# The same steps in another order: the step list of an attention and mixture-of-experts kernel

## The chip, the cores and the metric

The kernel runs on one core of a Trainium2 chip. The metric is the device time of one execution in microseconds (us). Five engines take part, each with its own queue of instructions that it works off in order: PE (TensorE, matmuls), DVE (VectorE), ACT (ScalarE), POOL (GpSimd) and SP (SyncE, which here issues nearly all DMA transfers).

## The reference

Linear attention with positive features (batch 4, 8 heads, 576 tokens, 64 dimensions a head, 128 features), then two layers of experts. In each, a gate picks one of 8 experts for each of the 2304 tokens.

```python
def phi(x):
    proj = np.einsum('bhsd,md->bhsm', x, omega)
    h = proj - np.sum(x * x, axis=-1, keepdims=True) / 2.0
    h = h - np.max(h, axis=-1, keepdims=True)
    return np.exp(h) / np.sqrt(m)
kv = np.einsum('bhsm,bhsd->bhmd', k_p, v)          # k_p = phi(k * scale)
z = np.sum(k_p, axis=2)
num = np.einsum('bhsm,bhmd->bhsd', q_p, kv)         # q_p = phi(q * scale)
den = np.einsum('bhsm,bhm->bhs', q_p, z)[..., None] + 1e-06
x = num / den                                       # then (2304, 512)
# each expert layer: N = 2304, D = 512, E = 8, F = 1024
e_idx = np.argmax(x @ w_gate, axis=1)
for e in range(E):
    mask = e_idx == e
    h = np.maximum(x[mask] @ w1[e], 0.0)
    out[mask] = gate_w[mask, None] * (h @ w2[e])    # layer 1: also * sigmoid(x @ w_output_gate)[:, e]
```

## The kernel before, in words

Attention works on 16 pairs of heads, four to a batch. The expert layers work on eight units, one for each layer and batch, in the order (layer 0, batch 0), (0,1), (1,0), (1,1), (0,2), (0,3), (1,2), (1,3). A unit runs the batch's most frequent expert over all 576 tokens. For precision each weight and each activation is split into a high and a low part and each product is three matmuls. Tokens whose expert is another one are left over; here they fit in one small block of 32, which is computed apart and added into the outputs.

**The step list.** Nothing in the program but the string `PLAN` (line 47) sets the order. A loop takes its words one after the other and issues what each names; so the list gives each engine's queue its order, and an engine waits when the next instruction of its queue is not ready. Instructions on different engines run at the same time as far as their data allow. A digit issues so many steps of the experts' stream; a step is six matmuls on PE (line 91). A unit has 64 steps, called here `E0.0` to `E7.63` (unit, then step). The first 32 go up: after every second step ScalarE makes `hh` (line 514) and VectorE `hl` (line 515) out of one of two PSUM buffers, which PE needs again. The other 32 go down: after every fourth step VectorE multiplies a buffer by the gate weights into `y` (line 533).

A word with `+` does its copy on VectorE, without it on ScalarE (line 128). The letters, p standing for the pair (a hexadecimal digit):

| word | what it issues |
|---|---|
| `ap`, `bp`, `cp` | SP: loads of q, k, v of the pair |
| `qp`, `r`, `t`, `s`, `x` | PE projects q; copies of it to `qhh`; POOL's maximum over partitions (`qhl`, line 225); VectorE subtracts (line 229); ScalarE's exp |
| `kp`, `m`, `e`, `v`, `w` | PE projects k; VectorE's row maximum `nm` (line 194); ScalarE's exp; PE's k v sums; copy `kvr` |
| `n`, `d`, `f`, `g`, `h`, `l`, `o` | PE's numerator; VectorE divides; PE transposes; copy `xraw`; high copy, low part, store |
| `Fui`, `Hui`, `Lui` | SP loads piece i of unit u's weights (512 KB into one of two `wr` buffers); copy to `wh`; VectorE's `wl` (line 487) |
| `Gu`, `Pu`, `Wu` | the gate of unit u in eleven parts; its expert's number to SP; the load of gate weights |
| `Xuc`, `Yuc`, `Suc0` | high copy, low part for the next layer; store of a piece of `y` |
| `A` | the left-over block in 34 parts: VectorE's scans pick its tokens (lines 627 to 649: `scan`, `scan2`, `sel`), POOL gathers, PE computes (`pu`, `pyc`, `pby`), VectorE scales (`yw`), POOL scatters in eight copies (`by`, line 731) |
| `B` | the block added into an output that is already stored: loads, four adds on VectorE (line 752), stores |
| `Mucs` | the block added into a piece of unit 7's `y`, on VectorE (line 547); its store `S` follows |
| `I`, `J`, `T`, `zn` | set-up; loads of the gates; pools changed; n idle matmuls on PE |

The block belongs to one of two places, and a factor of one or zero decides whether `B` or `M` adds it; both are issued. `B` and `M` need all eight `by` copies. A wait of an instruction holds all that stands behind it on its engine.

Of the kernel before, what the change touches and what calls it, by code (L numbers as in the profile page):

```python
# [46 lines left out]
PLAN = """
a0 I a1 b0 b1 c0 c1 c2 J a2 a3 a4 b2 b3 b4 b5 c3 c4 c5 q00 q01 k00 r001 r010+ k01 r000 t00 r011+ m00 t01 q10 r101+
e000 e001 m01 r100+ s00 z8 q11 e010 e011 r111 r110 k10 x00 m10 k11 s01 t11 m11 v00 v01 e100 q20 x01 w0+ r201+ e101
r200 e110 s11 e111 t10 n00 n01 q21 k20 a5 r211 r210 d00 d01 s10 x11 m20 v10 v11 x10 t20 f00 w1 e201 g00+ f01 k21 g01+  # L50
o0 m21 h0+ e200 s20 t21 q30 e211 e210 r301 r300 n10 n11 v20 v21 q31 x20 a6 s21 d10 k30 d11 w2 m30 r311 t31 l0 r310 x21
k31 q40 r400 r401+ e300 e301 t30 m31 n20 n21 e311 q41 e310 a7 d20 s31 r411 f10 g10 s30 f11 k40 x31 g11+ o1 m40 t41
r410 x30 d21 v30 v31 s41 h1 l1 e401 e400 k41 m41 b6 t40 w3 f20 g20 x41 f21 k50 g21 o2 m50 s40 e411 e410 n30 n31 v40
v41 c6 e500 h2+ e501 l2 w4 q50 q51 a8 x40 r500 r501 d30 r510 d31 r511 n40 n41 f30 d40 d41 g30 f31 k51 g31 b7 m51 o3 h3
t50 s50 t51 G0 e510 G0 e511 l3 k60 k61 G0 v50 v51 m60 e601 w5 G0 x50 b8 c7 e600 s51 x51 m61 G0 G0 z3 k70 e610 e611 G0
m70 P0 F00 F01 k71 m71 n50 v60 v61 e700 n51 c8 e710 e711 G0 w6 e701 d50 d51 f40 f41 G0 G0 G0 g40 g41 o4 v70 v71 f50
f51 H00+ L00 F02 g50 g51+ o5 W0 q60 q61 a9 H01 r600+ r611 r610+ 1 L01 F03 1 t60 2 s60 1 H02 1 x60 1 L02 F04 6 H03 1
L03 F05 2 H04 2 L04 F06 5 H05+ 1 L05 F07 3 H06+ c9 1 L06 3 w7 2 H07 1 L07 6 S000 1 r601+ 1 t61 2 s61 2 q70 q71 r711 aa
x61 r710 r701+ r700 1 t71 1 S010 n60 n61 s71 t70 d60 d61 1 x71 1 s70 1 h4+ 1 x70 l4 f60 f61 n70 n71 d70 d71 g60+ g61+
o6 h5 l5 2 f70 g70 f71 q80 q81 r801 ab g71+ G1 G1 o7 r800 r810 h6+ l6 h7+ l7 r811 1 G1 t80 G1 1 t81 S020 G1 G1 2 s80  # L60
G1 2 x80 P1 F10 F11 1 s81 1 G1 2 q90 q91 ac r911+ r910 S030 G1 G1 G2 H10+ G2 L10 F12 r900 k80 k81 H11 m81 t90 G2 1
e811 e810 L11 F13 1 s90 2 x90 2 H12 2 H13 L12 F14 2 L13 F15 7 H14+ 1 L14 F16 1 H15 2 L15 F17 6 H16 1 L16 4 H17 X00+
Y00 2 L17 1 m80 G1 W1 2 e800 e801 3 v80 v81 ca w8 X10 S100 X01 Y01 1 Y10 X02+ 3 Y02 X03 Y03 2 G2 1 r901+ 1 G2 G2 S110
t91 1 X11+ 1 G2 1 Y11 P2 F20 F21 s91 b9 1 G2 1 x91 2 x81 1 G2 n80 n81 X12 H20 Y12 d80 S120 G2 d81 1 L20 F22 1 H21+ 1
f80 f81 k90 k91 m90 L21 F23 m91 g80 g81+ o8 1 e900 e901 2 e911 e910 ba bb 2 S130 H22 1 L22 F24 X13+ 2 H23+ Y13 1 L23
F25 qa0 qa1 ka0 ra00 ad ra10 ka1 bc ta0 ma1 ma0 ra11+ ra01 1 ea11 ea10 1 sa0 ea00 ea01 1 ta1 1 H24 xa0 v90 v91 va0 va1
cb cc L24 wa F26 sa1 w9 kb0 kb1 kc0 mc0 xa1 mb1 bd mb0 1 ec01 ec00 1 eb10 eb11 1 eb01 eb00 G3 G3 n90 n91 na0 na1 vb0
vb1 d90 da0 da1 d91 cd qb0 qb1 ae rb10+ rb11+ rb00 rb01 wb 1 f90 f91 kd0 kd1 g90 g91 kc1 mc1 be tb0 sb0 o9 tb1 md1 bf
md0 1 ec11 1 xb0 sb1 fa0 ga0+ ed10 ed11 1 ed00 ed01 1 H25+ 2 fa1 qc0 qc1 af L25 F27 rc11 rc00+ ga1+ oa rc10 rc01 2 tc1
1 tc0 1 sc1 2 H26+ 1 xc1 sc0 ec10 1 L26 6 h8 H27+ 2 L27 l8 h9 l9 ha 1 la G2 W2 5 S200 8 S210 1 G3 G3 1 G3 G3 2 P3 F30  # L70
F31 G3 xb1 2 G3 1 nb0 nb1 G3 G3 G3 qd0 qd1 rd11 db0 db1 rd01+ rd10 rd00 1 fb0 S220 gb0+ H30 td1 fb1 1 H31 L30 F32 1
L31 F33 sd1 3 xd1 gb1+ ob 1 hb lb 2 H32 W3 S230 G4 G4 L32 F34 1 H33+ G4 G4 L33 F35 1 G4 G4 3 G4 1 P4 2 G4 vc0 vc1 vd0
vd1 G4 H34 ke0 L34 F36 ce me0 G4 ke1 me1 G4 wc+ cf wd+ 1 ee01 1 ee10 ee11 6 H35+ 2 L35 F37 6 H36 2 L36 F40 6 H37+ 2
L37 F41 6 H40 S300 2 L40 F42 6 S310 H41+ 2 L41 F43 6 S320 H42+ 2 L42 F44 6 W4 S330 H43+ 2 L43 F45 6 H44 2 L44 F46 6
H45+ 2 L45 F47 6 H46 2 L46 6 H47 2 L47 1 xc0 nc0 nc1 dc0 dc1 1 td0 sd0 1 fc0 fc1 qe0 gc0 qe1 gc1+ xd0 hc+ lc re00 re01
nd0 nd1 re10+ te0 re11+ dd0 oc dd1 ee00 ve0 ve1 we te1 1 se0 2 fd0 xe0 fd1 kf0 kf1 mf0 gd0+ gd1 S400 od se1 mf1 X40 1
ef00 hd+ ef01 1 qf0 qf1 rf10 rf11 rf00+ ef10 ld ef11 rf01 xe1 1 tf0 2 vf0 ne0 ne1 vf1 sf0 de0 de1 xf0 wf tf1 sf1 2 fe0
xf1 ge0+ fe1 ge1 oe nf0 nf1 df0 df1 he le 1 S410 1 ff0 gf0 ff1 gf1 of 1 hf+ lf G5 G5 T 1 G5 G5 1 G5 G5 2 G5 1 P5 F50
F51 1 S420 G5 3 G5 G5 G5 2 H50+ 1 L50 F52 1 H51 2 L51 F53 4 H52+ 1 L52 F54 2 H53+ 2 L53 F55 5 H54 1 L54 F56 3 H55+ 1
L55 F57 5 H56+ 1 L56 6 H57 Y40 G6 1 X41 G6 L57 Y41 X42 1 Y42 G6 G6 X43+ 1 W5 1 Y43 G6 G6 3 G6 1 P6 S500 F60 F61 G6 8  # L80
H60+ S510 2 H61+ L60 F62 1 L61 F63 5 S520 S430 2 H62 2 L62 F64 4 S530 H63 2 L63 G7 G7 F65 1 G7 5 H64+ 2 L64 F66 6 H65
G6 G7 G6 G6 1 W6 L65 F67 1 G7 G7 2 G7 1 P7 1 A 1 G7 1 A H66 2 G7 G7 G7 L66 F70 1 A 3 A 2 A H67+ X50 Y50 1 X51 1 Y51
X52+ 2 A 1 L67 F71 2 Y52 X53+ 1 H70 S600 1 A A A A A A 1 L70 F72 1 Y53 5 S610 H71 2 L71 F73 6 S620 1 A 2 H72+ A 1 L72
F74 3 A 1 S630 W7 H73 2 L73 F75 A A A A A A 6 H74+ 2 L74 F76 6 H75 2 L75 F77 3 A A A 1 A A 2 H76 2 L76 4 A A 1 A A 1 A
A A A H77+ B B B B B B B B B B B 1 B 1 L77 7 M700 S700 8 M710 8 M720 4 M730 3 S710 S720 S730 M731 S731
"""


# [862 lines left out]
```

## Time and profile before

| | us |
|---|---|
| three runs | 543.71, 543.93, 544.29 (median 543.93) |
| the profiled execution's own time | 542.09 |
| its span, first to last instruction | 540.3 |
| first matmul, first expert matmul | 4.16, 54.63 |
| last VectorE instruction ends | 535.15 |
| busy: PE, DVE, ACT, POOL | 527.4 (98%), 341.5 (63%), 192.3 (36%), 73.9 (14%) |
| granted clock of TensorE | 0.997 |

The span is 1.8 us shorter than the execution's own time. Busy PE means that at least one matmul is in flight. In the timeline and the chain a row's first two numbers are its start and its length in us; `x2` means that the row joins two instructions of a kind.

### The profile page before, as it was taken

To read this page: it belongs to the slowest core of one execution; us is meant where nothing else is said; L and a number is where in the kernel's file an instruction comes from. 1 tells how busy PE (TensorE), PEld (TensorE's weight loads), DVE (VectorE), ACT (ScalarE), POOL (GpSimd) and SP (SyncE) were. 2 spreads that over 40 slices of the span, in tenths; PEclk is the share of its full clock that TensorE was granted. 3 is DMA by queue.
4 is the path that set the end of the run, shared out by engine and by line. 5 is a ranking of instruction groups with operands and counts; after the bars stand their busy time and mean duration, and the time that the engine had idled before them with its cause. 6 is when DMAs were issued, how large, how long until landed. Compare 5 with 4: busy or idle time off the path is not lost.

```text
span 540.3 us, 12897 instructions
## 1 busy us (share of the span) xinstructions
PE 527.4 (98%) x5278; PEld 503.2 (93%) x5278; DVE 341.5 (63%) x772; ACT 192.3 (36%) x490; POOL 73.9 (14%) x68
## 2 busy tenths in 40 slices
...
GB/s 301 176 135 199 202 142 28 90 196 121 102 70 197 253 151 133 33 124 223 91 83 157 121 101 5 66 69 178 119 60 171 174 49 94 261 155 347 172 94 48
DMA packets 83954, 74.18 MB, mean 137 GB/s; under 512 B 14256, under 2 KB 68144, under 8 KB 83888
## 3 DMA queue, kind: packets, MB, share of 16 engines
...
q10 hardware_dynamic: 288, 0.13, 0.1%
...
## 4 chain that ended last, share of the span: by engine, by line
PE 87%; DVE 8%; DMA 2%; ACT 1%; issue 1%; POOL 1%; POOLq 0%; DVEq 0%
PE pm L91 72%; PE ph L218 3%; PE pn L267 3%; PE ph L184 3%; PE pkv L241 2%; DVE nm L194 2%; PE pg L338 1%; DVE qhh L229 1%; PE pf L303 1%; DMA wr<-w1a 1%; DVE xt L289 1%; DMA om<-omst 1%; DVE wl L487 1%; ACT kp L198 0%; DVE old L752 0%
## 5 line engine op out<-in xcount | busy, mean ns | idle before, releaser
L91 PE MATMUL pm<-hh,wh 128*128 128x288 f32 x512 | 153.6, 300 | 0.3 <-DVE y L533 0.3
L91 PE MATMUL pm<-xh,wh 128*128 128x288 f32 x512 | 153.0, 299 | 0.3 <-DVE hl L515 0.3
L91 PE MATMUL pm<-xh,wl 128*128 128x288 f32 x512 | 151.0, 295 | 0.0
L91 PE MATMUL pm<-hh,wl 128*128 128x288 f32 x512 | 150.9, 295 | 0.0
L91 PE MATMUL pm<-hl,wh 128*128 128x288 f32 x512 | 150.8, 294 | 0.0
L91 PE MATMUL pm<-xl,wh 128*128 128x288 f32 x512 | 150.8, 294 | 0.0
L515 DVE SCALAR_TENSOR_TENSOR hl<-pm,hh 128x288 fp32r<-128x288 f32 x128 | 58.5, 457 | 84.5 <-ACT hh L514 84.2
L225 POOL PARTITION_ALL_REDUCE qhl<-qhh x32 | 65.9, 2099 | 284.0 <-DVE qhh L130 99.7
L514 ACT ACTIVATE hh<-pm 128x288 fp32r<-128x288 f32 x128 | 52.7, 413 | 136.2 <-PE pm L91 136.1
L91 PEld LDWEIGHTS pm<-xh,wh 128*128 128x128 f32 x512 | 96.1, 188 | 3.8 <-issue 1.4
L91 PEld LDWEIGHTS pm<-hh,wh 128*128 128x128 f32 x512 | 96.1, 188 | 3.3 <-issue 1.8
L91 PEld LDWEIGHTS pm<-hl,wh 128*128 128x128 f32 x512 | 96.1, 188 | 0.0
L91 PEld LDWEIGHTS pm<-xl,wh 128*128 128x128 f32 x512 | 96.1, 188 | 0.0
L91 PEld LDWEIGHTS pm<-xh,wl 128*128 128x128 f32 x512 | 96.0, 188 | 0.0
L91 PEld LDWEIGHTS pm<-hh,wl 128*128 128x128 f32 x512 | 96.0, 188 | 0.0
L487 DVE TENSOR_TENSOR wl<-wr,wh 128x1024 fp32r<-128x1024 f32 (+1 forms) x72 | 79.2, 1112 | 2.7 <-ACT wh L132 2.2
L533 DVE TENSOR_TENSOR y<-pm,cb 128x288 f32<-128x288 f32 x64 | 29.0, 455 | 69.6 <-PE pm L91 64.2
L132 ACT CAST wh<-wr 128x1024 fp32r<-128x1024 f32 (+1 forms) x39 | 36.9, 961 | 52.2 <-PE pm L91 32.6
L198 ACT ACTIVATE kp<-ph,nm 128x128 f32<-128x128 f32 x140 | 39.4, 386 | 13.1 <-DVE nm L194 13.1
L194 DVE TENSOR_REDUCE nm<-ph 128x3 f32<-128x384 f32 (+1 forms) x64 | 27.7, 483 | 4.7 <-PE ph L184 4.7
L229 DVE TENSOR_TENSOR qhh<-qhh,qhl 128x576 f32<-128x576 f32 x32 | 28.9, 905 | 1.0 <-POOL qhl L225 0.9
L233 ACT ACTIVATE qhh<-qhh 128x576 f32<-128x576 f32 x32 | 22.1, 696 | 15.3 <-DVE qhh L229 15.3
(128 smaller groups left out, 431.2 us busy)
## 6 DMA issues: line engine op xcount, KB each, us to landing
...
```

What stands on the lines that cost most here:

```text
L91: nc.tensor.matmul(out, ws(*t), xs(*t), start=first and t == terms[0], stop=last and t == terms[-1])
L132: nc.scalar.copy(out=out, in_=in_)
L184: nc.tensor.matmul(pk[j][:, i * NF : (i + 1) * NF], self.kr[r, c0 : c0 + 128], om[r, :], start=True, stop=True)
L194: nc.vector.tensor_reduce(out=nm[:, j, 0:m], in_=pk, axis=AX.X, op=ALU.max, negate=True)
L198: nc.scalar.activation(self.kp[:, c, j * NF : (j + 1) * NF], self.pk[part][j][:, i * NF : (i + 1) * NF], AF.Exp, bias=self.nm[part][:, j, ...
L225: nc.gpsimd.partition_all_reduce(qm, qe, 128, bass_isa.ReduceOp.max)
L229: nc.vector.tensor_tensor(out=qe, in0=qe, in1=qm, op=ALU.subtract)
L233: nc.scalar.activation(qe, qe, AF.Exp)
L487: nc.vector.tensor_tensor(out=wl[:, p], in0=self.raw[i][:, p], in1=wh[:, p].bitcast(F32), op=ALU.subtract)
L514: nc.scalar.activation(hh[:, s], pm, AF.Relu)
L515: nc.vector.scalar_tensor_tensor(out=hl[:, s], in0=pm, scalar=0.0, in1=hh[:, s].bitcast(F32), op0=ALU.max, op1=ALU.subtract)
L533: nc.vector.tensor_tensor(out=y[:, t], in0=pm, in1=self.cb[:, t], op=ALU.mult)
```

## The change

The string `PLAN` is replaced; every other line is the same. Both lists hold the same words, except that `z3` becomes `z7` and that the `+` of 64 copies is set or taken away, in all about as often; words for single steps and whole groups of them stand elsewhere. The beginning, the place in unit 6 and the end, of which the prediction speaks, in core (the line breaks mean nothing):

```diff
-a0 I a1 b0 b1 c0 c1 c2 J a2 a3 a4 b2 b3 b4 b5 c3 c4 c5 q00 q01 k00 r001 r010+ k01 r000 t00 r011+ m00 t01 q10 r101+
-e000 e001 m01 r100+ s00 z8 q11 e010 e011 r111 r110 k10 x00 m10 k11 s01 t11 m11 v00 v01 e100 q20 x01 w0+ r201+ e101
...
-k31 q40 r400 r401+ e300 e301 t30 m31 n20 n21 e311 q41 e310 a7 d20 s31 r411 f10 g10 s30 f11 k40 x31 g11+ o1 m40 t41
...
-f51 H00+ L00 F02 g50 g51+ o5 W0 q60 q61 a9 H01 r600+ r611 r610+ 1 L01 F03 1 t60 2 s60 1 H02 1 x60 1 L02 F04 6 H03 1
...
-x61 r710 r701+ r700 1 t71 1 S010 n60 n61 s71 t70 d60 d61 1 x71 1 s70 1 h4+ 1 x70 l4 f60 f61 n70 n71 d70 d71 g60+ g61+
...
-F74 3 A 1 S630 W7 H73 2 L73 F75 A A A A A A 6 H74+ 2 L74 F76 6 H75 2 L75 F77 3 A A A 1 A A 2 H76 2 L76 4 A A 1 A A 1 A
-A A A H77+ B B B B B B B B B B B 1 B 1 L77 7 M700 S700 8 M710 8 M720 4 M730 3 S710 S720 S730 M731 S731
+a0 I q00 b0 r000 q01 r010 t00 r001+ r011+ a1 a2 k00 b1 b2 m00 J e000 q10 r100+ k01 t01 r101+ z8 q11 e001 c0 m01 k10
+e010 r111 k11 e011 s00 x00 m10 c1 v00 s01 t11 r110 e100 m11 v01 c2 q20 x01 w0+ n00 e101 n01 e110 s11 t10 b3 b4 c3
...
+m21 e200 s20 e211 n11 h0+ q30 t21 s21 e210 q31 r301 b5 v20 r300 v21 r310 x21 d10 x20 k30 w2 q40 r311 r401 k31 d11 m30
...
+c8 F02 g50 f51 g51 H01+ L01 q60 q61 r611 1 r610 2 r600 t60 1 F03 H02+ 2 L02 3 G0 H03+ 1 L03 4 h4 1 F04 H04+ F05 4 r601
+3 a8 a9 H05+ 2 W0 2 L04 F06 c9 3 t61 s61 1 L05 2 x61 2 o4 2 F07 3 o5 1 l4 1 H06 L06 H07 5 s60 x60 L07 S000 h5+ q70 q71
+r701 r700+ 1 l5 1 n60 S010 n61 r710+ r711 t71 d60 s71 d61 x71 3 t70 s70 x70 1 f60 f61 g60 g61+ h6 n70 n71 d70 1 d71 1
...
+1 X03 1 Y10 X11 Y11 2 v80 v81 ca w8 G2 G2 S100 Y03 X12 n80 d80 n81 d81 Y12 H20 S120 4 H21+ f80 f81 qa0 g80 g81+ k90
...
+ed00 2 fa0 ga0+ H25 L25 ed01 1 F27 1 tb1 sb1 fa1 qc0 rc00 qc1 rc10+ rc11+ 1 rc01 1 tc0 2 tc1 1 G3 1 G3 1 be 1 ga1+ 3
...
+H67 L67 5 F70 F71 1 X53+ 4 A A A A H70 Y53 A L70 F72 H71 L71 5 A A F73 A H72+ 4 L72 1 F74 1 H73 W7 L73 7 S630 1 H74 2
+L74 6 A A S600 2 F75 H75 1 F76 A A 8 L75 1 F77 11 H76+ H77 S620 9 L76 A A A A L77 1 A 2 A A 4 A A A 1 A A S610 1 A A A
+A 2 B B B B B B B B B B B B M720 2 M700 S720 M730 S700 S730 1 M710 2 M731 S710 S731
```

## Rows read from the trace of the kernel before

**Rows 1.** Table of stretches: us, then each engine's busy time, granted clock, DMA

```profile
4.16:54.60 50.44, 48.82 (x853) 39.96 (x853) 44.57 (x122) 40.48 (x132) 24.50 (x12) 1.00 0.62 207
...
54.60:92.00 37.40, 37.13 (x280) 36.66 (x278) 20.47 (x34) 12.15 (x24) 4.89 (x2) 1.00 0.42 127
...
512.00:534.00 22.00, 21.67 (x163) 21.31 (x161) 8.32 (x14) 0.00 (x0) 0.00 (x0) 1.00 0.27 101
```

**Rows 2.** Waits of PE: who <- released by, us in all, times, longest

```profile
PE ph L218 <- DVE om L816: 4.2, 1, 4.2
PE pn L267 <- ACT kp L198: 0.4, 1, 0.4
```

**Rows 3.** Timeline of PE, the first expert matmul: start, us, line, operands

```profile
54.63 0.40 PE L91 MATMUL pm<-xh,wh 128*128 128x288 f32 x1
```

**Rows 4.** Timeline of VectorE (DVE), 6 to 55 us; in brackets idle, releaser

```profile
6.49 0.82 DVE L130 COPY qhh<-ph 128x288 f32<-128x288 f32 x2 [2.38 <-PE ph L218]
...
7.95 1.02 DVE L194 TENSOR_REDUCE nm<-ph 128x3 f32<-128x384 f32 x2 [0.64 <-PE ph L184]
...
19.05 0.82 DVE L130 COPY xraw<-pf 128x384 f32<-128x384 f32 x2 [0.43 <-PE pf L303]
...
53.18 1.29 DVE L487 TENSOR_TENSOR wl<-wr,wh 128x512 fp32r<-128x512 f32 x2
```

**Rows 5.** Chain that ended last, 54 to 62 us: start, us, what

```profile
54.49 5.10 DMA wr<-w1a
...
59.62 1.05 ACT wh L132
...
61.52 0.54 PE pm L91 x2
```

**Rows 6.** Groups by line and shape: count, busy us, mean ns, idle before

```profile
L132 ACT CAST wh<-wr 128x1024 fp32r<-128x1024 f32 x31 | 32.5, 1048 | 41.7 <-PE pm L91 22.0 <-DMA wr<-w1b 14.2 <-DMA wr<-w1a 5.3
...
L130 DVE CAST wh<-wr 128x1024 fp32r<-128x1024 f32 x25 | 17.1, 684 | 0.4 <-DMA wr<-w2a 0.4
```

**Rows 7.** Timelines of POOL and VectorE, 93 to 100 us

```profile
93.83 3.91 POOL L225 PARTITION_ALL_REDUCE qhl<-qhh  x2 [3.52 <-ACT qhh L132]
...
95.83 1.71 DVE L229 TENSOR_TENSOR qhh<-qhh,qhl 128x576 f32<-128x576 f32 x1 [0.31 <-POOL qhl L225]
...
99.09 0.75 DVE L229 TENSOR_TENSOR qhh<-qhh,qhl 128x576 f32<-128x576 f32 x1
```

**Rows 8.** Timeline of VectorE, 510 to 530 us

```profile
510.19 3.01 DVE L752 SCALAR_TENSOR_TENSOR old<-by,state,old 128x576 f32<-128x576 f32 x4 [0.59 <-POOL by L731]
...
513.11 1.22 DVE L487 TENSOR_TENSOR wl<-wr,wh 128x1024 fp32r<-128x1024 f32 x1
...
528.28 0.82 DVE L547 SCALAR_TENSOR_TENSOR y<-by,state,y 128x576 f32<-128x576 f32 x1
```

**Rows 9.** Chain that ended last, 507 us to the end

```profile
507.16 0.12 PE pby L720
...
508.84 0.17 POOL by L731
...
509.10 0.55 POOL by L731
...
514.75 19.36 PE pm L91 x144
...
534.14 0.47 DVE y L533
...
534.63 0.52 DVE y L547
```

**Rows 10.** Timeline of VectorE, 460 to 477 us

```profile
460.20 1.34 DVE L627 TENSOR_TENSOR_SCAN order<-ones 128x576 f32<-128x576 f32 x1
...
471.96 0.51 DVE L632 TENSOR_SCALAR sel<-bx,state 128x576 f32<-128x576 f32 x1
...
475.65 0.82 DVE L644 SCALAR_TENSOR_TENSOR sel<-order,state,sel 128x576 f32<-128x576 f32 x1
```

More of the change, by code (lines that the diff above doesn't have):

```diff
@@ L47 @@
 PLAN = """
-a0 I a1 b0 b1 c0 c1 c2 J a2 a3 a4 b2 b3 b4 b5 c3 c4 c5 q00 q01 k00 r001 r010+ k01 r000 t00 r011+ m00 t01 q10 r101+
-e000 e001 m01 r100+ s00 z8 q11 e010 e011 r111 r110 k10 x00 m10 k11 s01 t11 m11 v00 v01 e100 q20 x01 w0+ r201+ e101
-r200 e110 s11 e111 t10 n00 n01 q21 k20 a5 r211 r210 d00 d01 s10 x11 m20 v10 v11 x10 t20 f00 w1 e201 g00+ f01 k21 g01+
-o0 m21 h0+ e200 s20 t21 q30 e211 e210 r301 r300 n10 n11 v20 v21 q31 x20 a6 s21 d10 k30 d11 w2 m30 r311 t31 l0 r310 x21
-k31 q40 r400 r401+ e300 e301 t30 m31 n20 n21 e311 q41 e310 a7 d20 s31 r411 f10 g10 s30 f11 k40 x31 g11+ o1 m40 t41
@@ L53 @@
[L53 to L56, printed above, removed]
-f51 H00+ L00 F02 g50 g51+ o5 W0 q60 q61 a9 H01 r600+ r611 r610+ 1 L01 F03 1 t60 2 s60 1 H02 1 x60 1 L02 F04 6 H03 1
@@ L58 @@
-L03 F05 2 H04 2 L04 F06 5 H05+ 1 L05 F07 3 H06+ c9 1 L06 3 w7 2 H07 1 L07 6 S000 1 r601+ 1 t61 2 s61 2 q70 q71 r711 aa
-x61 r710 r701+ r700 1 t71 1 S010 n60 n61 s71 t70 d60 d61 1 x71 1 s70 1 h4+ 1 x70 l4 f60 f61 n70 n71 d70 d71 g60+ g61+
-o6 h5 l5 2 f70 g70 f71 q80 q81 r801 ab g71+ G1 G1 o7 r800 r810 h6+ l6 h7+ l7 r811 1 G1 t80 G1 1 t81 S020 G1 G1 2 s80
-G1 2 x80 P1 F10 F11 1 s81 1 G1 2 q90 q91 ac r911+ r910 S030 G1 G1 G2 H10+ G2 L10 F12 r900 k80 k81 H11 m81 t90 G2 1
-e811 e810 L11 F13 1 s90 2 x90 2 H12 2 H13 L12 F14 2 L13 F15 7 H14+ 1 L14 F16 1 H15 2 L15 F17 6 H16 1 L16 4 H17 X00+
@@ L63 @@
[L63 to L82, printed above, removed]
@@ L83 @@
-X52+ 2 A 1 L67 F71 2 Y52 X53+ 1 H70 S600 1 A A A A A A 1 L70 F72 1 Y53 5 S610 H71 2 L71 F73 6 S620 1 A 2 H72+ A 1 L72
-F74 3 A 1 S630 W7 H73 2 L73 F75 A A A A A A 6 H74+ 2 L74 F76 6 H75 2 L75 F77 3 A A A 1 A A 2 H76 2 L76 4 A A 1 A A 1 A
-A A A H77+ B B B B B B B B B B B 1 B 1 L77 7 M700 S700 8 M710 8 M720 4 M730 3 S710 S720 S730 M731 S731
+a0 I q00 b0 r000 q01 r010 t00 r001+ r011+ a1 a2 k00 b1 b2 m00 J e000 q10 r100+ k01 t01 r101+ z8 q11 e001 c0 m01 k10
+e010 r111 k11 e011 s00 x00 m10 c1 v00 s01 t11 r110 e100 m11 v01 c2 q20 x01 w0+ n00 e101 n01 e110 s11 t10 b3 b4 c3
@@ new lines @@
+r201+ c4 r200 q21 e111 k20 r211 d00 d01 r210 v10 t20 v11 s10 x11 x10 w1 m20 f00 a3 a4 f01 g00+ k21 a5 n10 g01+ e201
+m21 e200 s20 e211 n11 h0+ q30 t21 s21 e210 q31 r301 b5 v20 r300 v21 r310 x21 d10 x20 k30 w2 q40 r311 r401 k31 d11 m30
+r400 q41 e300 l0 m31 c5 e301 t30 s30 e310 n20 r410 d20 n21 r411 a6 t31 e311 f10 g10 x30 s31 f11 k40 g11+ x31 k41 b6
+t41 h1 v30 v31 m40 d21 e401 o0 l1 s41 f20 e400 w3 f21 k50 t40 g20 m41 g21 n30 x41 e410 n31 m50 s40 e411 h2+ e501 e500
+o1 l2 v40 v41 q50 w4 x40 q51 o2 r500 r511 n40 n41 d30 r501 d31 f30 f31 r510 g30 g31 k51 b7 k60 d40 d41 a7 t50 c6 h3
@@ new lines @@
+m51 e510 e511 l3 m60 G0 G0 s50 G0 G0 k61 t51 e600 G0 s51 e601 m61 e611 v50 x50 G0 e610 v51 x51 k70 k71 b8 w5 G0 c7 m71
+e710 m70 e711 z7 n50 P0 f40 e700 f41 e701 F00 F01 G0 g40 g41 o3 n51 d50 v60 v70 v71 G0 G0 w7 v61 w6 d51 f50 H00+ L00
+c8 F02 g50 f51 g51 H01+ L01 q60 q61 r611 1 r610 2 r600 t60 1 F03 H02+ 2 L02 3 G0 H03+ 1 L03 4 h4 1 F04 H04+ F05 4 r601
+3 a8 a9 H05+ 2 W0 2 L04 F06 c9 3 t61 s61 1 L05 2 x61 2 o4 2 F07 3 o5 1 l4 1 H06 L06 H07 5 s60 x60 L07 S000 h5+ q70 q71
+r701 r700+ 1 l5 1 n60 S010 n61 r710+ r711 t71 d60 s71 d61 x71 3 t70 s70 x70 1 f60 f61 g60 g61+ h6 n70 n71 d70 1 d71 1
```

21 lines of the change are left out of this document (added).

## The prediction

> **What bounds the kernel now.** I read the table of stretches first: from 54.60 us on, PE is busy in 37.13 of 37.40 us and later in 21.67 of 22.00; before that, from 4.16 to 54.60, it is busy in 48.82 of 50.44, but VectorE is busy in 44.57 there, against 20.47 of 37.40 in the next stretch [rows 1]. The list of PE's waits comes second: 4.2 us for `om` at the start, which no list of steps can move, and otherwise nothing over 0.4 us in one line [rows 2]. The kernel thus has two regimes. From the first expert matmul (54.63) to the last [rows 3] PE streams, and only holes can be won. Before it, PE's busy time is padded: its matmuls are pipelined and count as busy while a small attention matmul waits for its successor. Adding the spacing of the same matmuls where they run undisturbed gives me some 43 us of PE work for the 50.4 us (an estimate, put together from the timeline). VectorE, 44.57 busy, has an idle rest of 5.9 in the table, but the timeline has its work for the first expert from 6.49 to 54.47, and within that its real holes sum to 2.3 us, the largest 0.64 and 0.43 [rows 4]. So VectorE sets the first expert matmul.
>
> The profiled execution took 542.09 us, with a span of 540.3; the median of the runs shown is 543.93, 1.84 more. I sum differences against the span and lay them on the median.
>
> **The change, part by part.** The same steps are issued, so no instruction is added but four idle matmuls (z3 becomes z7) of 0.11 us spacing, 0.44 us, in a stretch where PE has some 7 us to spare (50.4 less 43): nothing; if that cover were gone, 0.44. The other edits are "+" signs, which send copies to VectorE or ScalarE, and places in the list.
>
> *Up to the first expert matmul.* VectorE's ordered work before it shrinks: `r401` loses its "+", and that copy of 128x288, half of the 0.82 us that two take [rows 4], goes to ScalarE, 0.37 us by spacing; `L01` and `H01` now stand ahead of the first digit, but behind `L00`, for which alone that digit waits. The list also begins with `q00` and puts `r001+` before the first k step, where before it came after k00. VectorE's first copy stood at 6.49, behind eight query matmuls; behind the first four it can start at about 5.5. That lead of 0.9 shrinks to about 0.65 by my walk through the order of both engines up to the copies that now start at 19.05 [rows 4], since there `g00+` waits for PE's matmuls instead. After that both orders keep VectorE filled. Gain 0.4 + 0.65, of which I give back 0.25 for the holes of the new order: **-0.8**. Bounds: all 2.3 us of holes, the 0.37 and 0.3 of smaller moves gone gives -3.0; a VectorE as hungry as in the two largest holes of before, once more, gives +1.0.
>
> *Between.* Adding the gaps between PE's matmuls after 54.63, I find stalls of some 2.5 us in all. The first is typical: the eighth expert step starts only at 61.52, 0.4 late, because the 512 KB load of `wr` lands at 59.59, ScalarE makes `wh` of it in 1.05, and `hh` and then `hl` queue behind that [rows 5]. In the new list `H02`, `H03` and `H04` bear a "+": on VectorE the same cast takes 0.684 against 1.048 [rows 6], and no `hh` stands behind it. This stall, 0.4 and 0.2 in the next two steps, should go. The second is in the chain of q7: VectorE's `qhh` at 95.83 took 1.71 instead of 0.75, because it lay beside POOL's reductions [rows 7]; with `s71` ahead of `t70` in the new list most of 0.5 goes. The third is before `E7.40`, the 41st step of the last unit: `wl` behind four adds [rows 8], then y, and PE at 514.75 [rows 9], 0.6; its adds are moved away from there. The small rest, 0.8, I count as gone too where its steps are moved, since I find none of those orders again.
>
> New holes come. Between `E6.55` and the y of `E6.59` (the 56th and 60th step of unit 6) VectorE now has `scan`, `scan2`, `sel` and `H72+`: 1.34, then 4.51 with one y of 0.46 in it [rows 10], and 0.68, 6.1 us together, while PE has eight steps, 6.4 us, before it needs the bank that this y empties. With `L70` and `L71` (1.22 each, as the `wl` in [rows 8]) just before, I take 0.5 of stall. `n80` waits for its kv copy `w8`, with only one small matmul between: 0.3. In unit 2 `sb1`, `rc10+` and `rc11+`, all on VectorE, stand before an `hl`, and ScalarE's kp activations before an `hh`: 0.4, about what the same kind of queue cost in [rows 5]. With 0.2 left of q7 and 0.5 for what I have not seen, 1.9 against 2.5: **-0.6**. Ends: -2.0 if none of the new holes opens but the unseen, +1.5 if each named one is twice as large (2.8) and the unseen 1.2.
>
> *The tail.* Before, the left-over tokens' block was done by PE in the first half of the last unit: `pby` ended at 507.28, POOL's eight `by` copies ended at 510.15, and the four adds ran from 510.19 [rows 8, 9], with the last 24 steps (19.36 us) still to come. In the new list `pyc` stands right before `E7.55` and `pby` right behind it, the adds (`B`) behind `E7.58`, and then come `M720`, `M700`, `M730`, `M710` and `M731`, each adding the block into an output. All of that is VectorE's, in this order, with the y of `E7.59` and `E7.63` between. Let T be the start of `E7.55`, a step at 19.36/24 = 0.807.
> PE: nine steps and `pby` (0.12) end at T + 7.38. If PE set the end, y and `M731` would follow as before, in 0.03 + 0.47 + 0.02 + 0.52 = 1.04 [rows 8, 9]: T + 8.42.
> VectorE: `pby` ends at T + 0.93. From there to the first add took 507.28 to 510.19, 2.91, but one of the eight copies took 0.55 instead of 0.17 [rows 9] while VectorE cast a `wh`; no cast stands beside it now, so 2.53 to 2.91. The adds start at T + 3.46 to 3.84. Four take 3.01, and the next instruction started 2.92 after the first of them [rows 8]. Four of 0.82 would be 3.27: each begins some 0.08 before the one ahead has ended. Then M 0.74, y 0.38, M 0.74, the half M 0.43, M 0.74, y 0.38 and the half M 0.52: 3.93. End T + 10.3 to 10.7, against 8.42: **+1.9 to +2.3, I take +2.1**. The stores behind it are as before: `M731` ended at 535.15 and the program at 540.3, and I keep these 5.15. Nothing hides this tail, since PE has no work behind `E7.63`. It would be +1.2 if the first adds could run beside POOL's last copies for 0.9, which their wait for `by` forbids; that is the lower end, and +2.8 the upper, if each of the dozen instructions waited 0.05 more.
>
> On the shared port, the Trainium skill ("SBUF — State Buffer", section "Who interferes with whom") says that a VectorE instruction with two SBUF inputs, or a copy in its two-port mode, and a POOL instruction that reads SBUF exclude each other for the whole instruction. The copy of 0.55 agrees: it ended when the cast did. The `qhh` of 1.71 does not: it ended at 97.54, ahead of the reductions' 97.74, where the whole exclusion would have kept it until about 98.5.
>
> Sum: -0.8 - 0.6 + 2.1 = **+0.7**, span 541.0, the profiled execution's like 542.8, on the median **544.6 us**.
>
> **Rivals.** (1) *The fill of VectorE wins.* If the new order closes all its holes before the first expert matmul, that matmul comes 3.0 earlier, and with -0.6 and the tail's +2.1 the sum is -1.5; with half of the new holes, 0.95, absent, -2.4: 541.5 us. For it: VectorE is the bound there, and 2.3 us of holes are there to be closed. Against: after 20 us there are few, and short, and PE's own chain follows close. It decides if the first expert matmul starts before 52.5.
> (2) *No gain at the start: slower.* PE, not VectorE, sets the copies `g00+`, and the lead dies there, as it does once in [rows 4] where VectorE waits 0.43 for pf. Then 0 - 0.6 + 2.1 = +1.5: 545.4 us. It decides if the first expert matmul is not before 54.4.
> (3) *Collisions with POOL: slower.* Each two-input instruction on VectorE that starts beside a reduction costs 1.71 - 0.75 = 0.96 [rows 7]. Steps s and t have been moved against each other throughout; three more such collisions where a chain has no slack give +2.9, with the sum 547.5 us. Against: I find as many neighbours as before, and most lie under PE's stream. By the Trainium skill's whole exclusion (same page and section) a collision would cost up to the reduction's length, about 1.96, and the three some 5.9; no row shows that length lost.
> (4) *The list does nothing.* PE's stream stays its 480 us long, new holes replace old ones, and the end follows PE: 543.9. It needs the adds and merges to fit beside the last steps, and against that stands the tail's own chain.
>
> **How the numbers follow.** About 0.2%, 1.09 us, is what a measurement of this kernel can tell from no change: below 542.84 is faster, above 545.02 slower. My forecast, with (4) inside it, has 0.45 and its own range is 543.3 to 545.6; 0.10 of it lies above 545.02. Rival 1 has 0.30, 0.02 of it within the bound; rival 2 has 0.17, 0.03 within; rival 3 has 0.08. Faster 0.28, same 0.35 + 0.02 + 0.03 = 0.40, slower 0.10 + 0.14 + 0.08 = 0.32. The range takes rival 1 with a little more than its -2.4, -2.9, and rival 3 whole: 541.0 to 547.5.
>
> **What would show it.** The first expert matmul (`E0.0`) should start near 53.8; VectorE's first copy near 5.5. The stall at the eighth step of unit 0 and that before `E7.40` should be missing, and PE should wait before `E7.0` and `n80`. After the last matmul VectorE should work on without a hole: y and M for about 3.1 us (1.04 + 2.1) where it was 1.04. I am wrong if VectorE's last chain ends within 1.5 us of the last matmul, or if PE's gaps after `E0.0` sum to over 4 us.

## The result and the profile after

The changed list is slower. Its six runs have a median of 547.85 us (546.32 to 548.41) against 543.40 (542.73 to 544.29) for six of the kernel before; the recorded ratio is 1.0086, with a 95% interval of 1.0071 to 1.0101 (the two medians alone give 1.0082). Run again beside later experiments it had 1.0090 (1.0074 to 1.0107). The forecast was 544.6, in a range of 541.0 to 547.5: the time lies above it by 0.35, and 3.3 us above the forecast. The profiled execution has a span of 545.9 us, 5.6 over that of before.

The page's first lines and its chain by engine, after:

```profile
span 545.9 us, 12875 instructions
...
PE 528.4 (97%) x5282; PEld 504.7 (92%) x5282; DVE 340.5 (62%) x774; ACT 190.5 (35%) x488; POOL 72.0 (13%) x68
...
PE 87%; DVE 6%; ACT 2%; DMA 2%; issue 1%; POOL 0%; POOLq 0%; DVEq 0%; ACTq 0%
```

PE's busy time is up by 1.0, the other engines' is down. Most of the loss is waiting, and the waits of PE say where some of it is (who <- released by, us in all, times, longest):

```profile
PE ph L218 <- DVE om L816: 4.4, 1, 4.4
PE pc L380 <- DVE top L365: 0.9, 1, 0.9
...
PE pm L91 <- DVE y L533: 0.5, 1, 0.5
PE pn L267 <- ACT kvr L132: 0.4, 2, 0.2
```

The 4.2 us of [rows 2] became 4.4, which is the load of `om`: over the 17 profiles of this study the wait ends between 3.85 and 4.5 us, with any list. The wait of `pc` is new; it lies in the start. `E7.0` waits 0.5 for a y, as forecast.

The next fences show the stretches that changed: the table of stretches (us, then busy time of PE, PEld, DVE, ACT, POOL, clock, DMA share, GB/s), which answers to [rows 1], PE's first expert matmul [rows 3], and VectorE's beginning [rows 4].

```profile
4.41:56.75 52.34, 49.94 (x858) 41.47 (x858) 45.95 (x122) 41.08 (x134) 23.82 (x12) 1.00 0.58 187
56.75:63.21 6.46, 6.46 (x50) 6.46 (x49) 3.82 (x6) 2.22 (x6) 1.96 (x1) 1.00 0.56 174
535.59:539.83 4.24, 0.96 (x8) 0.73 (x6) 4.20 (x8) 0.00 (x0) 0.00 (x0) 0.86 0.80 295
539.83:545.90 6.07, 0.00 (x0) 0.00 (x0) 0.00 (x0) 0.00 (x0) 0.00 (x0) 0.50 0.36 132
```

```profile
56.75 0.40 PE L91 MATMUL pm<-xh,wh 128*128 128x288 f32 x1
```

```profile
5.81 0.46 DVE L130 COPY qhh<-ph 128x288 f32<-128x288 f32 x1 [1.46 <-PE ph L218]
6.77 0.46 DVE L130 COPY qhh<-ph 128x288 f32<-128x288 f32 x1 [0.50 <-PE ph L218]
8.01 1.02 DVE L194 TENSOR_REDUCE nm<-ph 128x3 f32<-128x384 f32 x2 [0.78 <-PE ph L184]
...
19.56 0.82 DVE L130 COPY xraw<-pf 128x384 f32<-128x384 f32 x2 [0.28 <-PE pf L303]
```

The start, from the first matmul to the first expert matmul, takes 52.34 instead of 50.46. VectorE does begin earlier (5.81 for 6.49, with a first matmul 0.25 later), but it spends most of the lead in holes of 0.50 and 0.78 by 8.01. The eight expert steps behind the start run without a gap (6.46 for 6.89, from 54.63 to 61.52 before). The end is a stretch of 4.24, the last step and what follows, in which VectorE is busy and PE only for the first 0.96, where 2.01 stood before (533.15 to 535.15), and then 6.07 in which no engine computes, where 5.15 stood.

VectorE's end, which answers to [rows 8] and [rows 9]:

```profile
530.50 0.28 DVE L723 TENSOR_TENSOR yw<-pby,xg 128x128 f32<-128x128 f32 x1
532.92 3.01 DVE L752 SCALAR_TENSOR_TENSOR old<-by,state,old 128x576 f32<-128x576 f32 x4 [2.14 <-POOL by L731]
535.84 0.81 DVE L547 SCALAR_TENSOR_TENSOR y<-by,state,y 128x576 f32<-128x576 f32 x1
536.57 0.45 DVE L533 TENSOR_TENSOR y<-pm,cb 128x288 f32<-128x288 f32 x1
536.94 1.97 DVE L547 SCALAR_TENSOR_TENSOR y<-by,state,y 128x576 f32<-128x576 f32 x3
538.83 0.45 DVE L533 TENSOR_TENSOR y<-pm,cb 128x288 f32<-128x288 f32 x1
539.31 0.52 DVE L547 SCALAR_TENSOR_TENSOR y<-by,state,y 128x288 f32<-128x288 f32 x1
```

From the adds' start to the end VectorE has no hole: this is the chain of the prediction, instruction by instruction. What the prediction did not have is the part of the stores, which SP issues (SPq is its queue; start, us until the row's last issue ends):

```profile
533.76 3.67 SPq L754 DMA_DIRECT2D outT<-old  x4
537.48 3.57 SPq L556 DMA_DIRECT2D outT<-y  x5
...
539.86 1.19 SPq L556 DMA_DIRECT2D outT<-y  x1
```

The last row is the issue of the last store. Before, it took 0.33 (535.18 to 535.51); now SP needs 1.19 us for the same instruction, the last of nine stores that it issues from 533.76 on. In the first two rows four issues take 3.67, with waits for the adds in them, and five take 3.57, the last row's among them. The long issue is not there in every execution: in the seven profiles with the late chain the last store's issue took 1.19 to 1.23 in three and 0.33 to 0.39 in four. In all seven this store landed late, 3.8 to 4.2 us after its issue began, where the ten profiles without the late chain have 1.7 to 3.2. The last store of before, of after and of run `i2`, which is after once more (KB, us to landing):

```profile
outT<-y SPq DMA_DIRECT2D x1, 144.0 KB, 1.9
...
outT<-y SPq DMA_DIRECT2D x1, 144.0 KB, 3.9
...
outT<-y SPq DMA_DIRECT2D x1, 144.0 KB, 4.2
```

### The profile page after: what moved, and what is told of

Its sections match the earlier page's. It is cut to its first block, busy times and chain, and to the rows that moved or that the text cites. A ratio compares the mean times of both kernels' runs of the same rounds, so it can differ in the third digit from the quotient of the medians.

```text
span 545.9 us, 12875 instructions
## 1 busy us (share of the span) xinstructions
PE 528.4 (97%) x5282; PEld 504.7 (92%) x5282; DVE 340.5 (62%) x774; ACT 190.5 (35%) x488; POOL 72.0 (13%) x68
## 4 chain that ended last, share of the span: by engine, by line
PE 87%; DVE 6%; ACT 2%; DMA 2%; issue 1%; POOL 0%; POOLq 0%; DVEq 0%; ACTq 0%
PE pm L91 71%; PE ph L218 4%; PE pn L267 3%; PE pkv L241 3%; PE ph L184 2%; PE pf L303 2%; ACT kp L198 1%; PE pg L338 1%; DVE nm L194 1%; DMA wr<-w2b 1%; DVE qhh L229 1%; DVE wl L487 1%; DMA om<-omst 1%; DVE y L547 1%; ACT qhh L233 0%
## 5 line engine op out<-in xcount | busy, mean ns | idle before, releaser
L132 ACT CAST wh<-wr 128x1024 fp32r<-128x1024 f32 (+1 forms) x36 | 35.1, 979 | 41.8 <-PE pm L91 14.4
L233 ACT ACTIVATE qhh<-qhh 128x576 f32<-128x576 f32 x32 | 22.1, 700 | 28.0 <-DVE qhh L229 27.9
L218 PE MATMUL ph<-qr,om 64*128 64x288 f32 x128 | 24.0, 459 | 4.5 <-DVE om L816 4.4
```

The lines of the kernel that those rows point to most:

```text
L132: nc.scalar.copy(out=out, in_=in_)
L218: nc.tensor.matmul(ps[i], om[r, :], self.qr[r, tokens(s)], start=True, stop=True)
L233: nc.scalar.activation(qe, qe, AF.Exp)
```

## The experiments

All profiles of the study can be cut at the same named instructions, so each list gives several readings of a segment. The table is worked out from the traces: start is from the first matmul to `E0.0`, and n00-E0 the part of it from the first numerator matmul (`n00`, line 267) on; units 0-6 from there to `E7.0`, unit 7 to the start of `E7.63`, chain from there to VectorE's end, and last is the rest (the last store's issue and landing, then the program's close). The lead to the first matmul (3.85 to 4.50) is left out.

```
kernel                       start  n00-E0  unit 2  units 0-6  unit 7  chain  last
before                       50.46  40.29    73.81    423.13    55.40   2.01  5.15
e3_before_new_end            50.84  40.25    73.84    423.13    54.54   4.23  5.98
h3_before_end_block_earlier  50.01  40.28    73.81    423.97    56.34   2.01  5.48
h4_before_two_edits          50.80  40.25    73.82    422.72    54.78   2.01  5.04
e2_new_old_start             50.65  40.29    74.09    427.32    54.63   4.24  6.44
after                        52.34  41.95    75.28    424.20    54.63   4.24  6.05
i2_changed_again             52.01  42.01    74.42    423.35    54.63   4.24  6.17
e1_new_old_end               52.23  42.00    75.94    424.86    56.06   2.00  5.13
g1_block_15_steps_earlier    53.19  43.11    74.07    422.98    58.30   2.01  5.07
g2_start_gate_order          51.25  41.50    74.06    422.98    54.63   4.24  5.73
g3_k30_earlier               51.98  42.00    74.07    423.00    54.63   4.24  5.58
g4_h24_later                 52.26  41.94    74.67    423.58    54.63   4.23  6.16
h1_block_7_steps_earlier     52.68  41.94    74.88    423.81    56.40   2.00  5.20
h2_three_edits               51.54  41.67    74.07    423.01    56.40   2.01  5.14
i3_block_7_steps_wl_ahead    51.83  42.00    74.06    422.98    54.69   2.01  5.11
i1_three_edits_wl_ahead      51.66  41.68    75.75    424.66    54.67   2.01  5.00
e4_before_new_start          51.99  41.99    73.81    425.05    55.39   2.01  5.17
```

Up to `n00` the profiles differ by 1.0 us, whatever the list: it starts 9.73 to 10.74 us after the first matmul. PE's first matmuls run at half their later pace (those of line 184 0.207 us apart, then 0.105), and the later the pace changes, the later is `n00`; the trace's first record of the full granted clock, the upper of the two levels of 1.2 and 2.4 GHz, stands at that change, between 7.0 and 10.4 us. Behind `n00` a list repeats itself: 40.25 to 40.29 with the start of before, 41.94 to 42.01 in seven of the eight profiles with the changed one. (The eighth, g1, had PE at the lower clock for a while; last section.) So the changed start loses 1.7 us, all of it behind `n00`, which stands here before and after:

```profile
14.33 1.39 PE L267 MATMUL pn<-kvr,qhh 128*64 128x65 f32 x40
...
14.80 1.39 PE L267 MATMUL pn<-kvr,qhh 128*64 128x65 f32 x40
```

**First, the list in halves.** The two lists were joined at `E7.0` and at `E0.0`, steps that one half lacked put at the joint.

```diff
 # e1: changed list
-<the changed list from E7.0 on>
+<the list of before from E7.0 on>
 # e3: list of before
-<the list of before from E7.0 on>
+<the changed list from E7.0 on>
```

> The changed list, but from E7.0 on the list of before (A, B, M and S of the last unit at their old places). Theory: the late left-over block costs 2.2 us on VectorE and another 0.9 us in the issue of the last stores on SP, and 0.8 us of it is given back in the unit's steps. The kernel then ends 3.1 - 0.8 = 2.3 us earlier than the changed one: about 3.3 us over the kernel before in the profile, with VectorE's last instruction 1.0 us behind the last matmul. Rival: the tail merely shows lateness made earlier, and the time stays within 1 us of the changed kernel's, 5.6 us over in the profile.

Measured: ratio 1.0053 (1.0036 to 1.0070), span 544.6. The chain is 2.00 and last 5.13, as the theory has it; unit 7 is 56.06 instead of 55.4, since the joint left a stall of 0.71 at `E7.4`, and unit 2 lost 1.9 (below). Nearer to the theory than to the rival, by size not clean.

> The list of before up to E7.0, then the new list. Theory: slower than before by 3.1 - 0.8 = 2.3 us, with VectorE ending 3.2 us after the last matmul and the last store's issue taking about 1.2 us. Rival (tail harmless by itself): within 0.5 us of before.

Measured: 1.0042 (1.0028 to 1.0056), 2.3 us; chain 4.23, last 5.98, unit 7 faster by 0.86. The end alone makes the kernel slower, by what was worked out. This run also says something of the start, which is that of before: half of the first piece of weights landed late, VectorE's `wl` ended 0.47 us behind the start of `E0.0`, and `E0.0` stood where it stands in the other profiles of this start, 40.25 behind `n00`.

```profile
54.24 1.29 DVE L487 TENSOR_TENSOR wl<-wr,wh 128x512 fp32r<-128x512 f32 x2
...
55.06 0.40 PE L91 MATMUL pm<-xh,wh 128*128 128x288 f32 x1
```

```diff
 # e2: changed list
-<the changed list up to E0.0>
+<the list of before up to E0.0>
 # e4: list of before
-<the list of before up to E0.0>
+<the changed list up to E0.0>
```

> The changed list, but up to E0.0 the list of before. Theory: the new beginning costs 1.9 to 2.1 us; the first expert matmul is back at 54.6 and the end comes 1.9 us earlier than the changed kernel's, about 3.6 us over the kernel before. Rival: PE's stalls of the first unit take the lateness up, as the changed kernel's profile has regained 1.2 us of it by E1.0, and only about 0.9 us is won.

Measured: 1.0107 (1.0077 to 1.0136). The start is back at 50.65, 1.7 less, but unit 0 lost 4.3: at the joint SP's queue had a store, the load of the gate weights and a q load ahead of the load of a weight piece, which then landed at 66.11, and PE waited 2.7 us in the middle of the unit. So the total decides nothing; the start's own reading does.

> The new list up to E0.0, then the list of before. Theory: the first expert matmul comes at 56.5 to 56.8, 1.9 to 2.1 us late, and the whole kernel is slower by that. Rival (regained in the first unit): slower by 0.7 to 1.0.

Measured: 1.0052 (1.0036 to 1.0068), 2.8 us. The start reads 51.99, 1.5 over; another 1.6 came at `E0.16`, again a weight load behind the joint (landed at 68.71). Unit 0 as a whole took 65.43, 1.1 over before and not 1.6, since the wait before `E0.8` was missing; of the rival, a late start regained in the unit, nothing more is seen.

**Second, one edit of the changed list at a time.**

```diff
 # g2
-m60 G0 G0 s50 G0 G0 k61 t51 e600 G0 s51 e601 m61 e611 v50 x50 G0 e610 v51 x51
+m60 G0 G0 s50 x50 G0 G0 k61 t51 e600 G0 s51 x51 e601 m61 e611 v50 G0 l3 e610 v51
 # (and l3 taken away ahead of m60)
```

> The changed list with one edit at 41 to 49 us: the gate's part that puts ls on ScalarE stands behind s50 and x50, x51 right behind s51, and l3 at the end of the group. Theory: ScalarE's idle 2.05 us before ls goes (it waits for VectorE's top behind l3, m60, s50), n50 comes 1.2 us earlier and so does the first expert matmul: 55.5 instead of 56.75, and the time falls by 0.8 to 1.5. Rival: PE's own work behind n50 sets that matmul and VectorE is full anyway: under 0.4.

Measured: 1.0059 (1.0036 to 1.0082); start 51.25, 1.1 less than the mean of the eight profiles with the changed start (52.32). Of that, 0.45 fell before `n00`, where nothing was edited, and g1's slow clock is in the mean; behind `n00` the start reads 41.50, 0.5 less than 41.98, the mean of the other seven. The times do not single the edit out: g3 and g4 beside it have 1.0061 and 1.0065. The chain that ended last, after, shows what the edit went for (start, us, what):

```profile
42.28 1.39 DVE xl L321
43.67 0.93 DVE nm L194 x2
44.60 0.67 DVE qhh L229
45.27 0.14 DVE gt L364
...
45.74 0.26 ACT ls L366
46.00 2.05 ACT kp L198 x8
48.05 0.57 ACT qhh L233
...
49.13 0.57 ACT qhh L233
49.70 0.16 ACT kvr L132
...
49.91 0.92 PE pn L267 x24
```

The path runs through VectorE, then ScalarE, then PE. ScalarE had stood still for 2.05 us before `ls`:

```profile
43.42 0.28 ACT L343 COPY lg<-pg 128x144 f32<-128x144 f32 x1 [0.21 <-PE pg L338]
45.74 0.26 ACT L366 COPY ls<-pt 72x128 f32<-72x128 f32 x1 [2.05 <-DVE top L365]
```

In the run with the edit the hole is gone, and the two exps of q (L233) come at 43.05 and 44.76 instead of 47.91 and 48.98:

```profile
43.05 0.68 ACT L233 ACTIVATE qhh<-qhh 128x576 f32<-128x576 f32 x1 [0.28 <-DVE qhh L229]
43.83 0.26 ACT L366 COPY ls<-pt 72x128 f32<-72x128 f32 x1
...
44.76 0.69 ACT L233 ACTIVATE qhh<-qhh 128x576 f32<-128x576 f32 x1
```

Before, the same queue had `e601` ahead of `ls` and a hole of 1.32 ahead of that. Counted from `n00`, `ls` started only 0.28 us later after than before, but `n50`, PE's first numerator of pair 5, 1.76 later (35.11 for 33.35): between them stand the exps of k that the list of before had ahead of `ls`. With the edit `n50` comes 0.7 earlier and `E0.0` 0.5, under a third of the start's loss. The edit does not separate its parts: it also takes `l3` out from ahead of `top`, and `l3`'s `xl` stands in the chain above with 1.39, beside POOL's reductions; where it stands now it takes 0.75. And the path then meets the next limit. From 44.15 on PE has no wait up to `E0.0`, and the seven idle matmuls lie in this path (from the chain that ended last, g2):

```profile
47.48 0.87 PE idle L835 x7
48.35 0.85 PE pn L267 x24
```

In after they lie ahead of a wait for `kvr` and cost nothing. In g2 the four added ones come to some 0.5 us (an estimate, four sevenths of 0.87); no run took them out.

```diff
 # g3
-q31 r301 b5 v20 r300 v21 r310 x21 d10 x20 k30
+q31 r301 b5 k30 v20 r300 v21 r310 x21 d10 x20
```

> The changed list with one edit at 22 to 26 us: k30 ahead of v20, v21 on PE. Theory: VectorE's hole of 0.61 us ahead of m30 goes, and with VectorE as the bound the first expert matmul comes 0.5 earlier. Rival: the lead is lost again at the next wait for PE or in a collision with POOL, under 0.2 is left.

Measured: 1.0061 (1.0040 to 1.0081); start 51.98, and behind `n00` 42.00, within the 41.94 to 42.01 that the changed start reads without any edit. The edit wins nothing, as its rival had it.

```diff
 # g4
-H24+ L24 G2 v90 va0 va1 cb v91 cc wa sa0 w9 kb0 ... xa1 bd eb01 o8
+G2 v90 va0 va1 cb v91 cc wa sa0 w9 kb0 ... xa1 bd eb01 H24+ L24 o8
```

> The changed list with one edit in unit 2: H24+ and L24, behind whose 512 KB load VectorE waited 0.83 us, stand seven VectorE steps later, behind eb01. Theory: the row maxima and ScalarE's exps of pairs a, b and c come 2 us earlier, PE's stalls before na1 and f90 (0.80 and 0.19, 0.1) go, 1.0 us is won. Rival: E2.11's hh still stands behind nine exps on ScalarE and PE's stall only moves: under 0.3.

Measured: 1.0065 (1.0042 to 1.0088); unit 2 took 74.67, against 75.28 in the profile of after. But runs g1, g2 and g3, which do not touch that place, read 74.06 and 74.07. The hole that I meant to remove is in the execution and not in the list alone: VectorE's row of after,

```profile
187.57 0.69 DVE L130 CAST wh<-wr 128x1024 fp32r<-128x1024 f32 x1 [0.83 <-DMA wr<-w2b]
```

has waits of 0.98, 0.97 and 0.76 in i1, e1 and i2, 0.35 in g3 and none in g1 and g2, by how fast one load of 512 KB fell out, and unit 2 takes 74.1 to 75.9 with it: 74.1 in the six profiles where the load took 4.8 to 5.4 us, 74.4 to 75.9 in the five where it took 5.8 to 6.25. With the list of before, unit 2 read 73.8 in five profiles. The edit itself is not judged by this.

```diff
 # g1 (15 steps earlier; h1 the same at E7.40, 7 steps earlier)
-<pu .. by, B> between E7.47 and E7.59
+<pu .. by, B> from E7.32 on, S610 ahead of them
```

> The changed list with one edit: the last 16 parts of the left-over block and the adds B stand 15 steps earlier (pu at E7.32 instead of E7.47); M and S of the last unit stay, but S610 goes ahead of B. Theory: VectorE's chain behind the last matmul shrinks from 3.3 to 1.04 us and the last stores no longer queue on SP (0.9): 2.5 to 3.1 us earlier than the changed kernel, profile at 542.8 to 543.4. Rival: the end is late because PE's stream is late, and less than 1 us is won.

Measured: 1.0106 (1.0080 to 1.0131). The chain is 2.01 and last 5.07, 3.2 less together, but unit 7 took 58.30 instead of 54.63: `pu` waited 1.7 for a block's weight that landed at 509.30, and `E7.48` another 1.7, for `wl`. The end was cured and the stall moved.

> The changed list with one edit: the last 16 parts of the left-over block and B stand 7 steps earlier (pu at E7.40, its weights had landed by then in the run with 15 steps), S610 ahead of them. Theory: unit 7's steps stay at 54.6 us, VectorE's chain from the start of E7.63 to M731's end falls from 4.24 to 2.0 and the last store's issue follows within 0.4: 2.2 us less than the changed kernel, and up to 0.8 more where its stores queued. Rival: the stall moves into the unit's steps as it did with 15 steps, under 1 us is won.

Measured: 1.0049 (1.0034 to 1.0064). `pu` no longer waits, the chain is 2.00, and a stall of 1.85 is left in `E7.48`. It is my edit's: with the block, `L76` and `L77` had slipped behind `yw` on VectorE, as its timeline has it, and PE waited for that `wl`.

```profile
524.08 0.28 DVE L723 TENSOR_TENSOR yw<-pby,xg 128x128 f32<-128x128 f32 x1
524.28 2.35 DVE L487 TENSOR_TENSOR wl<-wr,wh 128x1024 fp32r<-128x1024 f32 x2
```

> The changed list with three edits: the block 7 steps earlier, the gate order at 41 to 49 us, and k30 ahead of v20. Theory: the start falls from 52.3 to about 50.8 us (before: 50.5 to 50.8), the end by 2.2; the sum is 3.7 us less than the changed kernel, at 0.0 to +0.8 us over the kernel before: the three places are what the change lost. Rival: a loss spread over many small moves, of which at least 1.5 us stays.

Measured: 1.0047 (1.0029 to 1.0066), with the same stall of 1.85; start 51.54 (41.67 behind `n00`), chain 2.01, last 5.14.

**Third, the end without that slip.**

```diff
 # i3: as h1, and
-L76 L77 behind E7.47, among the block
+L76 behind E7.41, L77 behind E7.45
 # i1: as i3, with the edits of g2 and g3
```

> The changed kernel itself once more, beside the two below. If the segments before were the list's own: start to first expert matmul 52.0 to 52.7, units 0 to 6 423.0 us plus 0 to 1.9 in unit 2 as the load of F24 falls, unit 7 54.6, the chain behind E7.63 4.24, and the last store's issue and the end together 5.6 to 6.2; ratio 1.007 to 1.010. Rival: the first profile was chance, ratio under 1.006.

Measured: 1.0090 (1.0074 to 1.0107), every segment inside what was expected; it was not chance.

> The changed list with the block 7 steps earlier, as in the run before, but L76 and L77 stand behind E7.41 and E7.45, ahead of yw. Theory: unit 7 takes 54.6, the chain behind E7.63 2.0, the store's issue and end 5.15: 2.2 + 0.8 = 3.0 us less than the changed kernel, ratio 1.003. Rival: another instruction holds y or wl behind the block and the 1.8 us stall stays.

Measured: 1.0022 (1.0008 to 1.0036): 0.68% or 3.7 us less than the changed list beside it by the ratios, 2.8 by the medians (543.78 and 546.60), where 3.0 was worked out. Unit 7 54.69, chain 2.01, last 5.11. VectorE and SP at the end:

```profile
524.70 3.01 DVE L752 SCALAR_TENSOR_TENSOR old<-by,state,old 128x576 f32<-128x576 f32 x4 [2.14 <-POOL by L731]
...
534.80 0.46 DVE L533 TENSOR_TENSOR y<-pm,cb 128x288 f32<-128x288 f32 x1 [0.85 <-PE pm L91]
535.29 0.52 DVE L547 SCALAR_TENSOR_TENSOR y<-by,state,y 128x288 f32<-128x288 f32 x1
```

```profile
535.84 0.33 SPq L556 DMA_DIRECT2D outT<-y  x1
```

The adds are the same 3.01 us, seven steps earlier; the last y waits for PE again, and the last issue takes 0.33.

> The same with the start's two edits. Theory: start 51.2 to 51.6 (before 50.5 to 50.8), units 0 to 6 423.0, unit 7 54.6, 2.0, 5.15: span 540.7 to 541.1, ratio 1.000 to 1.002, so that the three places are what the change lost. Rival: ratio over 1.003, a loss elsewhere that the profiles hide.

Measured: 1.0027 (1.0014 to 1.0041). Against i3 the runs show no gain from the start's two edits. Behind `n00` the profiles have 41.68 against 42.00, a gain of 0.3, but unit 2 read 75.75 against 74.06, so a difference of that size is beyond what these runs can tell. The expected 1.000 to 1.002 was missed. Of the 1.4 us that the start keeps over before (40.27), the four idle matmuls are an estimated 0.5; the rest is left open.

**Fourth, the other way round: what the list of before could still take.**

> The list of before up to E7.0, then the changed list with the block 7 steps earlier. Theory: unit 7 takes 54.6 us as in the changed list instead of 55.4, and the chain behind E7.63 takes 2.0 as before: 0.8 us faster than before. Rival: the adds beside wl and y stall PE as before, no gain.

Measured: 1.0018 (1.0006 to 1.0030), with the slip of h1 in it (unit 7 56.34). It shows nothing on its own theory.

```diff
 # h4: the list of before, in unit 0 and in unit 7
-E0.4 H02 E0.5 x60 E0.6 L02 F04 E0.7 E0.8 E0.9
+E0.4 E0.5 x60 E0.6 E0.7 H02 E0.8 E0.9 L02 F04
-H77+ B B B B B B B B B B B E7.32 B E7.33 L77 E7.34 E7.35
+H77+ L77 E7.32 E7.33 E7.34 E7.35 B B B B B B B B B B B B
```

> The list of before with two edits: H02 and L02 stand three steps later in unit 0, so that no hh waits behind a load on ScalarE, and L77 ahead of B with B behind E7.35. Theory: the stalls at E0.8 (0.43 and some 0.2 behind it) and at E7.40 (0.49 and 0.1) go: 1.0 to 1.2 us faster than before. Rival: hl behind L02, or y behind B, takes the place of each: no gain.

Measured: 0.9984 (0.9973 to 0.9996), 0.9 us faster than before: unit 0 63.89 for 64.33, unit 7 54.78 for 55.40. It beats both lists, by little.

## Why the prediction was wrong

The measured 0.86% is 4.7 us. The table gives it in parts, changed list less list of before:

| step of the prediction | forecast | measured |
|---|---|---|
| up to the first expert matmul | -0.8 | +1.8 (52.32, mean of eight, less 50.55, mean of five; 51.8 to 53.2 and 50.0 to 50.8); behind `n00` +1.7 (41.98 less 40.27) |
| between, units 0 to 6 | -0.6 with unit 7 | +0.45 (423.58, mean of ten, less 423.13; -0.15 to +1.7 as one load falls) |
| between, unit 7 | | -0.8 |
| the tail on VectorE | +2.1 | +2.23, the same in all seven profiles |
| what lies behind it | 0 | +0.9 (6.02, mean of seven, less 5.15, mean of ten) |
| sum | +0.7 | +4.6 |

**The step that failed** is "So VectorE sets the first expert matmul", with its -0.8. I added up VectorE's work and treated its order as the only one; my worst case for it was +1.0, and it lost 1.7. VectorE's own work for that matmul did not set it even before: in e3, with the same start, VectorE ended its part of `L00` 0.47 us behind `E0.0`, and `E0.0` came no later. What stands fast is PE's queue: from `n50` to `E0.0` it takes 6.74 to 7.07 us in all 17 profiles, so that `n50` decides, and before and after `n50` waits for ScalarE. In the changed list `ls` of the gate stands ahead of exps of k, waits for VectorE's `top` behind `xl`, `nm` and `qhh`, and PE's `n50` is 1.8 us later, counted from `n00` (35.11 for 33.35). VectorE's lead of 0.9 is gone where I had kept 0.65 of it, at the copies of 19.05: they start 14.96 us after the first matmul in the mean of the eight profiles, 15.00 in the mean of the five. Run g2 shows under a third of the loss, 0.5 of 1.7, with ScalarE's and VectorE's order edited together. The four idle matmuls, which I put at nothing, are an estimated 0.5 in the runs with that edit. Where the rest is was not found, and in the timed runs (i1 beside i3) the gain does not show.

**What lies behind the tail** I took over as 5.15 us from the profile of before. That assumed SP's issue at 0.33 and a last store that lands in 1.9. With the chain late, nine stores come within 6.1 us (533.76 to 539.86), and the last one lands 3.8 to 4.2 us after its issue began. In three of the seven profiles its issue itself took 1.2, in the other four the close behind a short issue took 5.2 to 5.5, where the ten without the late chain have 4.6 to 5.0. It is a term that I set to nothing, and it is 0.9. That the queue of stores causes it fits all profiles, with the late chain and without, but no run took the stores alone away.

**Between** had the right sign in unit 7 and at the named places: the eighth step's wait is gone (6.46 for 6.89 over the first eight steps), so is the one before `E7.40`, and the forecast holes are there: before `E7.0` with 0.65 for my 0.5, and before `n80` with some 0.3, as forecast (PE's matmuls 0.44 us apart where 0.13 is usual). Unit 2's holes I had at 0.4; between executions of the changed list the unit differs by 1.9 (74.06 to 75.94), and the long ones are those where VectorE's `H24+` waits longest for its load, with the row maxima of three pairs behind it. I had not seen that a "+" moves the wait for a load to the engine that everything else needs.

**The tail** was right as a mechanism and in size: the adds started at T + 3.90, just outside the T + 3.46 to 3.84 of the prediction, VectorE ended at T + 10.8 for 10.3 to 10.7, and the chain lost 2.23 for 2.1. e3 shows it in the list of before, and i3 takes it away.

**Rivals.** The second (no gain at the start, 545.4) came nearest, with a start that lost twice what it was to have gained. The third, collisions, came in a small part. Over the whole kernel they became fewer, but in the start before had a `qhh` of 1.63 and one of 1.04 where 0.75 is usual, and after has 1.72, 1.10 and the `xl` of 1.46. This last one, 0.7 over the usual, lies in the chain that leads to `n50`; how much of the loss is its, apart from the order, no run shows. No rival had a loss at the start, and none the stores.

The chances, 0.32 for slower, leaned too much on a net sum near nothing of three terms of which one, the start, had been walked on one engine only.
